# Products of the last third of each chunk cut by blocks of channels, with inverse units that wait for their own blocks and a new total order

## The chip, the cores and the metric

The kernel runs on one core of a Trainium2 chip. The metric is the device time of one execution in microseconds. An execution's time stands beside the span of its profile, which goes from the first to the last recorded instruction. Five engines run their own queues in order and wait for each other by semaphores: TensorE (PE, its weight loads shown as PEld), VectorE (DVE), ScalarE (ACT), GpSimd (POOL) and SyncE (SP), which here only issues DMAs.

## The reference

Two layers follow each other on a sequence of 2048 tokens of 640 channels (bf16):

```
k_shift = causal convolution of k with 4 taps per channel
kv      = k_shift * v
y       = irfft(rfft(kv padded to 4096) * rfft(ssm_k padded to 4096))[:2048]   # long convolution, per channel
h       = q + layernorm(q) * (y + kv * ssm_D)
out     = h + mish(layernorm(h) @ w1 + b1) @ w2                                # 640 -> 1728 -> 640
```

## The kernel before

The Fourier transforms are matmuls with constant tables, in two steps each way: 128 frequencies `f` by matmuls with cosine and sine tables, then 16 x 16 by a table `G` of its own for each `f`. The channels are taken in units of 128 ("dc", five of them) and grouped in three chunks: chunk 0 holds dc 0 and 1, chunk 1 dc 2 and 3, chunk 2 dc 4. Inside a chunk four channels form a group and four groups form a block of 16 channels, so chunks 0 and 1 have 16 blocks and chunk 2 has 8. The buffers `V` (transform of kv), `K` (transform of the filter) and `SW` (K with neighbouring partitions swapped, made by DMAs `sw0_*`, `sw1_*`, `sw2_*`) are laid out block by block, 128 frequencies x 4 groups = 512 elements for a block in a partition.

The stages, with the names that the order uses (`x` and `y` at the end of a name are the two halves of a unit):

- `k1pe`/`k1ev` and `ktpe`/`ktev` transpose the filter and k, `ktsh` shifts, `wsh` makes the small shift matrices on GpSimd, `kspe` makes k_shift in PSUM and `kv` (VectorE, L609) multiplies it by v.
- `s1kpe`/`s1kev` and `s1vpe`/`s1vev` (L558, L559) are the first forward step of filter and kv, 40 units each. They use TensorE as two tiles of 64 columns.
- `s2kpe`/`s2kev` (L658) and `s2vpe0`, `s2vpe1` with `s2vev0`, `s2vev1` (L693) are the second forward step: 43 units for the filter, 16 units for the kv of chunk 0 and 26 for that of chunks 1 and 2 together.
- `p2_c_i` (L718) multiplies SW by V and `p1_c_i` (L714) multiplies V by K in place, for piece i of chunk c. They run on VectorE or GpSimd.
- `i1pec_u`/`i1evc_u` (L751, L752) is the first inverse step, 16 + 16 + 8 units of 8 matmuls. Its result `Z` is written over `K`.
- `i2pa`, `i2pb`, `i2pc` (L809) are the second inverse step for the three chunks, 16 token tiles each. `y..a` and `y..b` take the results out, then come `wb`, `h`, `bn`, `pow`, `hc` (second layer norm), a transpose (`trpe`, or the DMA `trd`), `m1pe` (L906) with `hb` (Mish on ScalarE, L911), and `m2q`, `m2pe` (L927, L939) with `res` and `d_out`.

Every unit with a PE step allocates one of 8 PSUM banks, and its eviction (`..ev`, by ScalarE as L423 or by VectorE as L425) gives the bank back. `fz0` to `fz3` are four fillers of two 512-column matmuls on zeros, and `ln1_t` are the first layer norm's statistics of a token tile on VectorE.

Who does what, and in which order, is one list of words (`ORDER`, "name:engine"). `_schedule` walks over it and gives each operation a start time, and the instructions are emitted in the order of these times; on each engine this is the order of the list. Nothing is reordered at run time. Where GpSimd runs a product after one of VectorE, a one-column copy `turn` on GpSimd makes it wait for that product.

Three rules of the code matter to the change. In chunk 0 there are 8 pieces of 16 frequencies over all 16 blocks, in chunk 1 there are 4 pieces of 32 frequencies over all 16 blocks, and in chunk 2 there are 4 pieces of 32 frequencies over all 8 blocks. All units of the first inverse step of a chunk depend on all products of that chunk (`p_ops[c.i]`). And Z is laid out with each of its 32 rows over all channels of the chunk,

```
        Z.append(k.rearrange("p (j d) -> p j d", d=c.w))
```

so that what one unit writes is spread over the memory of all the blocks of K.

Of the kernel before, what the change touches and what calls it, by code (L numbers as in the profile page):

```python
# [26 lines left out]
d_id:s wz:v wm:t d_dr:s d_sk:s dcpe:t d_go:d d_n0:d d_n2:d k1pe0y:t warm:a k1ev0y:a d_n3:d dcev:v dq0:v k1pe0x:t k1ev0x:v cfpe:t k1pe2y:t s1kpe0_0y:t  # L27
s1kev0_0y:a s1kpe0_3y:t s1kpe0_2y:t s1kev0_3y:v s1kpe0_0x:t s1kpe0_1y:t dq3:v s1kpe0_3x:t s1kpe0_1x:t s1kpe0_2x:t dq2:v coef:a k1ev2y:a d_n1:d dq1:v
k1pe3x:t d_n4:d s1kev0_2x:a s1kev0_3x:v dq4:v d_k2:d wsh2_0:p kz:p wsh0_1:p wsh4_1:p wsh1_0:p wsh3_1:p wsh1_1:p wsh3_0:p s1kev0_1y:a k1pe1x:t k1pe1y:t
k1ev1y:a k1ev1x:v k1pe2x:t k1ev2x:v wsh4_0:p k1pe4y:t k1ev4y:v k1ev3x:v k1pe4x:t s1kev0_1x:a s1kpe1_1x:t k1pe3y:t s1kpe2_2x:t s1kev0_0x:a k1ev4x:a  # L30
d_k3:d s1kpe2_0x:t s1kev2_2x:a s1kev0_2y:a d_k0:d d_x0:d s1kpe2_0y:t s1kpe1_2x:t s1kev2_0x:a s1kpe4_3y:t s1kev2_0y:a s1kev4_3y:a k1ev3y:v s1kev1_1x:v
s1kev1_2x:v s1kpe3_0y:t s1kpe1_0y:t s1kpe1_0x:t s1kev1_0x:a s1kpe2_1y:t s1kpe3_3y:t s1kev3_0y:v s1kpe3_1y:t s1kev3_1y:a s1kev1_0y:a wsh2_1:p d_k1:d
d_g1:d d_g0:d s1kpe3_3x:t s1kev2_1y:v wsh0_0:p d_g2:d d_g7:d s1kpe2_1x:t s1kev2_1x:a s1kpe1_2y:t s1kpe1_1y:t fz2:t d_v1:d ln1_2:v s1kpe4_1y:t
s1kev4_1y:a ln1_3:v ln1p3:p ln1p2:p s1kev1_2y:v ktpe3y:t ktev3y:a s1kpe2_2y:t ktpe0y:t s1kev3_3x:a s1kev3_3y:a s1kev1_1y:v ln1_1:v fz0:t ktpe4y:t
# [20 lines left out]
s1vev2_2x:v s2kev_14y:v s1vev3_2x:v s2kpe_14x:t b1pe:t s1vev3_2y:a c_b1:a s1vpe4_3y:t s1vpe3_0y:t s2kev_14x:v s1vpe4_0x:t s1vev4_0x:a s1vev3_0y:v
p2_0_3:p p1_0_3:p d_x2:d sw0_2:d s2vpe0_6y:t s1vev4_1x:v p2_0_2:v s2vev0_6y:a s1vev4_3y:a s1vpe4_2y:t s1vpe2_2y:t s1vev4_2y:v s1vpe4_1y:t s1vpe4_2x:t
s1vev4_1y:v s1vpe3_3x:t s1vev2_2y:a s1vev3_3x:a s1vpe2_1y:t s1vev2_1y:a p2_0_7:p s1vpe3_1y:t s1vpe2_3y:t s1vev2_3y:v s1vpe2_1x:t s1vpe3_1x:t fz3:t
s1vev3_1x:a s1vev3_1y:a s1vpe2_3x:t s1vev2_3x:a s2vpe0_4y:t s1vev4_2x:a s2vpe0_4x:t s2vev0_4y:a s2vev0_4x:a s1vev2_1x:v s2vpe1_5y:t s2vpe1_6x:t
s2vpe1_8y:t s2vpe1_1x:t s2vev1_6x:a s2vev1_5y:a s2vpe1_4x:t s2vpe1_6y:t s2vpe1_3y:t s2vpe1_2y:t s2vev1_4x:a s2vpe1_1y:t p2_0_6:v sw1_0:d p1_0_7:v
p1_0_2:v p1_0_6:v s2vpe1_2x:t s2vpe1_8x:t s2vev1_6y:a s2vev1_2y:a p2_0_4:p s2vev1_8y:v sw1_1:d s2vpe1_4y:t s2vev1_1x:v s2vev1_1y:v s2vev1_3y:a  # L60
s2vev1_4y:a s2vpe1_5x:t fz1:t s2vpe1_11y:t s2vpe1_10x:t s2vev1_8x:v p2_0_5:v p1_0_4:v s2vpe1_0y:t s2vpe1_0x:t s2vpe1_3x:t s2vpe1_12x:t p1_0_5:v
s2vev1_5x:a s2vev1_2x:a s2vev1_3x:a sw2_1:d s2vpe1_11x:t s2vpe1_12y:t s2vev1_0x:a s2vev1_12x:a p2_1_1:v s2vev1_0y:a s2vpe1_9x:t p2_1_0:v p1_1_1:v
s2vev1_12y:a s2vev1_9x:a s2vev1_11x:a s2vev1_11y:a i1pe0_2x:t s2vpe1_9y:t i1pe0_7y:t s2vev1_9y:a p1_1_0:v i1pe0_5x:t s2vpe1_7x:t s2vev1_7x:a
s2vpe1_10y:t s2vev1_10y:a s2vpe1_7y:t s2vev1_7y:a i1pe0_2y:t i1pe0_0x:t i1pe0_4x:t p2_1_2:v s2vev1_10x:a i1ev0_0x:a i1pe0_5y:t p2_1_3:v p1_1_2:v
i1ev0_5x:a i1ev0_2y:a i1pe0_7x:t i1pe0_6x:t i1ev0_4x:a p1_1_3:v i1pe0_4y:t i1ev0_7x:a i1ev0_4y:a i1pe0_6y:t i1pe0_1x:t i1pe0_1y:t i1ev0_6y:a
i1ev0_2x:a i1pe0_3x:t i1ev0_7y:v i1pe0_0y:t i1pe0_3y:t i1ev0_3y:v i1ev0_1x:a i1ev0_1y:a i1pe1_4y:t i1pe1_3y:t i1ev0_0y:a i1ev1_4y:a i1ev0_5y:a
i1ev1_3y:a i1ev0_6x:a i1pe1_5x:t p2_2_3:v p2_2_2:v p1_2_3:v i1pe1_7y:t i1ev0_3x:a i1ev1_7y:a i1pe1_2y:t i1pe1_1y:t i1pe1_6x:t i1pe1_0x:t i1pe1_0y:t
i1pe1_5y:t i1ev1_5x:a i1ev1_0y:a i1ev1_1y:a i1pe1_7x:t i1ev1_7x:a i1ev1_6x:a sw2_0:d d_w11:d d_w14:d p2_2_1:v p2_2_0:v p1_2_2:v p1_2_1:v p1_2_0:v
d_t2m:d ln1_15:v d_w12:d i1pe1_4x:t i1pe1_3x:t i1pe1_6y:t i1pe2_3y:t i1ev1_4x:a d_w13:d i1ev1_0x:a i1ev1_5y:a i1pe1_2x:t i1pe2_3x:t i1ev1_2y:v
i1ev2_3x:v i1ev1_6y:v i1pe1_1x:t i1ev2_3y:a i1ev1_3x:a i1ev1_1x:v i1pe2_1y:t d_w10:d d_w2:d d_x1:d i1pe2_2x:t i1pe2_1x:t i1pe2_0x:t i1pe2_2y:t  # L70
# [222 lines left out]
def kernel(  # L293
# [698 lines left out]
```

## Time and profile before

| | before |
|---|---|
| median of 3 runs | 223.04 us (222.61 to 223.31) |
| profiled execution | 222.57 us, span 220.8 us |
| granted TensorE clock | 1.0 throughout |
| PE busy | 214.0 us, 97% of the span |
| VectorE busy | 144.1 us, 65% |
| ScalarE busy | 134.7 us, 61% |
| GpSimd busy | 73.0 us, 33% |

The shares are averages over stages of different kinds. Up to about 88 us TensorE, ScalarE and VectorE are all close to full; after about 110 us TensorE alone is. A TensorE that is busy for 97% of the span is not one that never waits: a matmul's end is modelled, and a matmul of 128 columns is shown as 220 ns long while the next one starts 55 ns later. What TensorE loses is therefore read from the distance between the starts of units of one kind.

### The profile page before, as it was taken

How to read it: one execution, taken by the hardware profiler on the slowest of the kernel's cores; microseconds unless marked ns; L12 is line 12 of the kernel's file. 1: busy time of each engine (PE TensorE's matmuls, PEld its weight loads, DVE VectorE, ACT ScalarE, POOL GpSimd, SP SyncE). 2: the span in 40 equal slices, each digit the busy share in tenths (PEclk: the TensorE clock that was granted, in tenths of full speed). 3: DMA queues.
4: the chain of work that ended last, by engine and by line, in shares of the span. 5: the costliest groups of instructions: out<-in, count | busy, mean ns of one | idle time of the engine just before them, and what ended most of it. 6: DMA issues, size and time to landing. Idle time of an engine off the chain costs nothing.

```text
span 220.8 us, 6315 instructions
## 1 busy us (share of the span) xinstructions
PE 214.0 (97%) x2626; PEld 158.3 (72%) x2626; DVE 144.1 (65%) x323; ACT 134.7 (61%) x264; POOL 73.0 (33%) x112
## 2 busy tenths in 40 slices
PE   7999999999988999999999999999999999999993
PEld 3997999898777999999776644567645444646672
DVE  0498999999999998999997999763500000020341
ACT  2699999999999999898773058600026655400000
POOL 0299983099740006025876451311000000000000
PEclk9999999999999999999999999999999999999999
DMA  6999992442999999603006300524350000000024
GB/s 216 405 415 406 423 404 96 98 93 57 286 261 277 325 390 359 200 0 62 0 0 62 62 0 0 75 46 92 89 149 1 0 3 0 0 26 7 0 82 155
DMA packets 32876, 31.03 MB, mean 141 GB/s; under 512 B 19024, under 2 KB 29264, under 8 KB 32464
## 3 DMA queue, kind: packets, MB, share of 16 engines
q1 hardware_dynamic: 32384, 30.43, 44.7%
q8 instruction: 20, 0.33, 0.6%
q10 hardware_dynamic: 368, 0.20, 0.4%
q14 instruction: 8, 0.07, 0.1%
q0 software_dynamic: 96, 0.00, 0.0%
HBM read 20.47 MB, written 2.62 MB: 105 GB/s over the span
## 4 chain that ended last, share of the span: by engine, by line
PE 79%; ACT 9%; DMA 7%; DVE 2%; issue 1%; SPq 0%
PE ps L939 26%; PE ps L906 26%; ACT uv L423 7%; DMA x<-in_A_q_dram 5%; PE ps L751 4%; PE ps L809 4%; PE ps L658 4%; PE ps L752 4%; PE ps L558 3%; DMA rn<-in_A_ssm_k_dram 2%; PE ps L605 2%; PE ps L693 2%; ACT uk L423 1%; PE ps L927 1%; PE ps L886 1%
## 5 line engine op out<-in xcount | busy, mean ns | idle before, releaser
L911 ACT ACTIVATE uv<-ps,b1s 128x512 bf16<-128x512 f32 (+1 forms) x65 | 35.8, 611 | 45.6 <-PE ps L906 37.6
L906 PE MATMUL ps<-G 128*128 128x512 bf16 (+1 forms) x325 | 58.9, 337 | 0.0
L939 PE MATMUL ps<-rn,uv 128*128 128x320 bf16 (+2 forms) x416 | 58.2, 299 | 0.0
L939 PEld LDWEIGHTS <-uv 128*128 128x128 bf16 x416 | 39.3, 98 | 17.9 <-issue 1.3
L423 ACT CAST uk<-ps 128x512 bf16<-128x512 f32 (+2 forms) x88 | 47.3, 707 | 2.7 <-PE ps L559 1.3
L906 PEld LDWEIGHTS <-G 128*128 128x128 bf16 x325 | 31.0, 98 | 24.4 <-issue 1.2
L423 ACT CAST uv<-ps 128x512 bf16<-128x512 f32 (+2 forms) x61 | 32.6, 769 | 0.0
L944 DVE TENSOR_TENSOR xa<-ps,xa 128x320 bf16<-128x320 f32 x12 | 5.8, 487 | 37.6 <-PE ps L939 37.6
L425 DVE CAST uk<-ps 128x512 bf16<-128x512 f32 (+1 forms) x35 | 21.8, 666 | 1.9 <-PE ps L559 1.4
L944 DVE TENSOR_TENSOR xb<-ps,xb 128x320 bf16<-128x320 f32 (+2 forms) x12 | 5.6, 488 | 21.0 <-PE ps L939 21.0
L751 PE MATMUL ps<-a,uv 128*128 128x128 bf16 x160 | 19.0, 219 | 0.2
L833 POOL TENSOR_TENSOR r<-ve,mhalf 128x1 f32<-128x1 f32 x16 | 9.7, 613 | 26.3 <-DVE ve L830 26.3
L751 PEld LDWEIGHTS <-uv 128*128 128x128 bf16 x160 | 17.9, 114 | 0.2 <-issue 0.2
L718 POOL TENSOR_TENSOR rn<-rn,uv 128x1024 bf16<-128x1024 bf16 x5 | 10.6, 2129 | 9.1 <-ACT uv L423 8.8
L425 DVE CAST uv<-ps 128x512 bf16<-128x512 f32 (+1 forms) x21 | 13.3, 677 | 0.1
L693 PE MATMUL ps<-uv,G 128*128 128x64 bf16 (+1 forms) x256 | 12.2, 197 | 1.2 <-issue 0.9
L658 PE MATMUL ps<-uk,G 128*128 128x160 bf16 x128 | 12.7, 230 | 0.4 <-ACT uk L423 0.3
L609 DVE TENSOR_TENSOR ra<-ps,rb 128x512 bf16<-128x512 f32 x20 | 12.5, 682 | 0.1
L693 PEld LDWEIGHTS <-G 128*128 128x128 bf16 x256 | 10.7, 96 | 2.2 <-issue 1.5
L559 PE MATMUL ps<-cst,ra 128*64 128x128 bf16 x160 | 10.9, 221 | 0.0
L558 PE MATMUL ps<-cst,ra 128*64 128x128 bf16 x160 | 10.8, 220 | 0.0
L809 PE MATMUL ps<-uk,ra 128*128 128x256 bf16 (+1 forms) x96 | 10.6, 255 | 0.0
(114 smaller groups left out, 377.3 us busy)
## 6 DMA issues: line engine op xcount, KB each, us to landing
G<-tab_g SPq DMA_DIRECT2D x8, 512.0 KB, 11.2
rn<-in_A_ssm_k_dram SPq DMA_DIRECT2D x5, 512.0 KB, 5.9
ra<-in_A_k_dram SPq DMA_DIRECT2D x4, 640.0 KB, 10.3
rb<-in_A_v_dram SPq DMA_DIRECT2D x2, 1280.0 KB, 10.2
G<-in_B_w_dram SPq DMA_DIRECT2D x5, 432.0 KB, 7.8
rn<-in_B_w_dram SPq DMA_DIRECT2D x1, 2080.0 KB, 12.6
rn<-uk SPq DMA_DIRECT2D x8, 256.0 KB, 4.2
rb<-uk SPq DMA_DIRECT2D x8, 256.0 KB, 5.0
```

Of the source, the lines that this page charges most:

```text
L423: nc.scalar.copy(o, i)
L425: nc.vector.tensor_copy(o, i)
L558: nc.tensor.matmul(ps[0:64, k, :], lhs, mc, start=True, stop=True)
L609: nc.vector.tensor_tensor(kv_w[:, m, k:32:2, 8 * h:8 * h + 8, :], ps.rearrange("p (l t d) -> p d t l", l=4, t=8), raw_v[:, 8 * h:8 * h + 8 ...
L658: nc.tensor.matmul(ps[:, o:o + 160], g_v[:, f, :], KA[:, :, f, :], start=True, stop=True)
L693: nc.tensor.matmul(ps[:, fl * n:fl * n + n], g_v[:, f0 + h * kf + fl, :], VX[x][:, :, f0 + h * kf + fl, :], start=True, stop=True)
L751: nc.tensor.matmul(pz[:, k, :], V[c.i][:, dg // 4, :, dg % 4], a12[:, 0, :], start=True, stop=False)
L809: nc.tensor.matmul(py, t2m[:, t2, ri, :], Z[c.i][:, ri * NT + t2, :], start=(ri == 0), stop=(ri == 1))
L906: nc.tensor.matmul(ph[:, 0:w], w1[:, dc, fc * P:fc * P + P], lnhT_of(u)[:, dc, 0:w], start=(dc == 0), stop=(dc == NDC - 1))
L911: nc.scalar.activation(hb_of(u)[:, fc, 0:w], rt.tile[:, 0:w], ACT.Mish, bias=b1s[:, fc:fc + 1], scale=1.0)
L939: nc.tensor.matmul(po[:, 0:d1 - d0], hb_of(u)[:, fc, tl * P:(tl + 1) * P], w2[:, fc, d0:d1], start=False, stop=(fc == NFC - 2))
L944: nc.vector.tensor_tensor(x, rt.tile[:, 0:d1 - d0], x, ALU.add)
```

## The change

The change cuts the last pieces of each chunk by blocks instead of by frequencies, lets each half unit of the first inverse step wait for the products of its own block alone, and lays Z out block by block, so that a half unit writes over the K block that it alone replaces. The second inverse step then reads its 256 (or 128) channels as runs of 16 that stand 512 elements apart. The rest is a new list `ORDER`: the same 411 TensorE operations and the same DMAs, in another order, and with other engines for some evictions and products. A piece in `PIECES` gives the first and last frequency and the first and last block, and `p_by` collects the products of each block.

```diff
+PIECES = [
+    [(16 * i, 16 * i + 16, 0, 16) for i in (0, 1, 2, 3)] + [(64, 96, 0, 8), (64, 96, 8, 16)] + [(16 * i, 16 * i + 16, 0, 16) for i in (6, 7)],
+    [(0, 32, 0, 16), (32, 64, 0, 16)] + [(64, 128, 4 * i, 4 * i + 4) for i in range(4)],
+    [(0, 64, 0, 4), (0, 64, 4, 8), (64, 96, 0, 8), (96, 128, 0, 8)],
+]
...
-        Z.append(k.rearrange("p (j d) -> p j d", d=c.w))
+        Z.append(k.rearrange("p (b j d) -> p b j d", j=2 * NT, d=16))
...
-        npf = (16, 32, 32)[c.i]
-        for i in range(P // npf):
-            f0, f1 = i * npf, (i + 1) * npf
+        for i, (f0, f1, b0, b1) in enumerate(PIECES[c.i]):
+            parts = [(max(b, b0) - b, min(b + t.shape[1], b1) - b, b, t) for b, t in SW[c.i] if b < b1 and b + t.shape[1] > b0]
...
+                    v = V[c.i][:, b0:b1, f0:f1, :]
+                    eng.tensor_tensor(v, v, K[c.i][:, b0:b1, f0:f1, :], ALU.mult)
...
+                for x, y, b, t in parts:
+                    k = t[:, x:y, f0:f1, :]
+                    eng.tensor_tensor(k, k, V[c.i][:, b + x:b + y, f0:f1, :], ALU.mult)
...
+            for b in range(b0, b1):
+                p_by[c.i][b] += [p2, p1]
...
-                ev(e, Z[c.i][:, :, d0:d0 + 4 * n].rearrange("p j (g l) -> p j g l", l=4), ps.rearrange("p (g j l) -> p j g l", g=n, l=4))
-            o_pe, o_ev = unit(f"i1pe{c.i}_{gi}", f"i1ev{c.i}_{gi}", 0.9, EV, 1024, p_ops[c.i] + [d_a12], pe, evf)
+                ev(e, Z[c.i][:, 2 * gi + h].rearrange("p j (g l) -> p j g l", l=4), ps.rearrange("p (g j l) -> p j g l", g=4, l=4))
+            o_pe, o_ev = unit(f"i1pe{c.i}_{gi}", f"i1ev{c.i}_{gi}", 0.9, EV, 1024, (p_by[c.i][2 * gi] + [d_a12], p_by[c.i][2 * gi + 1] + [d_a12]), pe, evf)
...
-                        nc.tensor.matmul(py, t2m[:, t2, ri, :], Z[c.i][:, ri * NT + t2, :], start=(ri == 0), stop=(ri == 1))
+                        nc.tensor.matmul(py, t2m[:, t2, ri, :], Z[c.i][:, :, ri * NT + t2, :], start=(ri == 0), stop=(ri == 1))
```

From the new order, the parts that the prediction uses. VectorE around the products (`:v` only, with `:p` for GpSimd's):

```
before  p2_0_6 p1_0_7 p1_0_2 p1_0_6 s2vev1_8y s2vev1_1x s2vev1_1y s2vev1_8x p2_0_5 p1_0_4 p1_0_5 p2_1_1 p2_1_0 p1_1_1 p1_1_0
        p2_1_2 p2_1_3 p1_1_2 p1_1_3 i1ev0_7y i1ev0_3y p2_2_3 p2_2_2 p1_2_3 p2_2_1 p2_2_0 p1_2_2 p1_2_1 p1_2_0 ln1_15
        i1ev1_2y i1ev2_3x i1ev1_6y i1ev1_1x i1ev2_1x i1ev2_2x i1ev2_2y y0a
before  GpSimd: p2_0_0 p1_0_0 p2_0_1 p1_0_1 p2_0_3 p1_0_3 p2_0_7 p2_0_4 gate
after   s2vev0_4y p2_0_7 s2vev1_11y s2vev1_7y s2vev0_5y s2vev1_4y s2vev1_8y p2_0_5 p1_0_7 p2_0_4 p1_0_6 p1_0_5 p1_0_4 s2vev1_11x
        p2_1_0 p1_1_0 p2_1_1 p2_1_2 p1_1_1 p1_1_2 p2_1_4 p2_1_5 i1ev1_0x p1_1_4 p1_1_5 p2_1_3 p2_2_3 p1_1_3
        p2_2_1 p2_2_2 p1_2_3 p1_2_1 p1_2_2 p2_2_0 p1_2_0 i1ev1_7x i1ev1_4y i1ev1_5y i1ev2_0y i1ev2_0x y0a
after   GpSimd: p2_0_2 p1_0_2 p2_0_3 p1_0_3 p2_0_0 p2_0_1 p1_0_1 p1_0_0 p2_0_6 gate
```

SyncE's DMAs up to the last token load:

```
before  d_n0 d_n2 d_n3 d_n1 d_n4 d_k2 d_k3 d_k0 d_x0 d_k1 d_g1 d_g0 d_g2 d_g7 d_v1 d_v0 d_g6 d_g4 d_g5 d_g3 d_a12
        sw0_0 sw0_1 sw0_3 d_x2 sw0_2 sw1_0 sw1_1 sw2_1 sw2_0 d_w11 d_w14 d_t2m d_w12 d_w13 d_w10 d_w2 d_x1
after   d_n0 d_n1 d_n2 d_n3 d_n4 d_k3 d_x0 d_a12 d_k2 d_k0 d_k1 d_g2 d_g3 d_g4 d_g1 d_v1 d_v0 d_g0 d_g7 d_g5 d_g6
        sw0_1 sw0_0 sw2_0 sw0_3 sw0_2 sw1_0 sw1_1 d_t2m sw2_1 d_w13 d_w11 d_w14 d_w12 d_w10 d_w2 d_x2 d_x1
```

TensorE's inverse units and their neighbours:

```
after   .. s2vpe1_12y fz1 fz0 s2vpe1_10y s2vpe1_9y fz3 s2vpe1_7x s2vpe1_8x s2vpe1_6y i1pe0_5y i1pe0_0x i1pe0_4y s2vpe1_6x i1pe0_2x
        s2vpe1_5x (11 more of i1pe0) i1pe1_0x 1x 0y 1y i1pe0_7y i1pe1_4x 5x 6x 6y 5y 7x 3x 7y 2x 3y 2y 4y
        i1pe2_2x 3x 2y 1x 0y i2pa0 i1pe2_1y 0x 3y i2pb0 i2pa1 i2pa8 i2pb1 i2pc0 ..
before  .. the last four s2vpe1 between the first i1pe0, then i1pe0, i1pe1 and i1pe2 in turn, i2pa0 i1pe2_0y i2pb0 i2pa1 i2pa2 i2pb1 i2pc0 ..
```

More of the change, by code (lines that the diff above doesn't have):

```diff
@@ L31 @@
[L31 to L34, printed above, removed]
@@ L55 @@
[L55 to L58, printed above, removed]
@@ L59 @@
[L59 to L70, printed above, removed]
@@ L572 @@
     p_ops = [[] for _ in CHUNKS]
+    p_by = [[[] for _ in range(c.ng // 4)] for c in CHUNKS]
     ks_pe_all, kv_ops, s1_k = [], [[] for _ in range(NDC)], {}
```

140 lines of the change are left out of this document (77 added, 63 removed).

## The prediction

> **What bounds the kernel now.** I read the page first (engine shares and slices), then the busy times by stage, then the timelines of ScalarE, VectorE, TensorE and GpSimd where the inverse step begins. Of these times, "start to start" means the distance between two starts in a timeline, since the durations shown overlap.
>
> The busy times by stage (columns: stretch, its length, then busy us and instructions of PE, PEld, DVE, ACT, POOL, then clock, DMA share, GB/s):
>
> ```profile
> 30.00:62.00 32.00, 31.06 (x720) 28.32 (x718) 31.75 (x54) 31.65 (x68) 19.84 (x17) 1.00 0.58 155
> 62.00:72.50 10.50, 9.79 (x181) 8.90 (x181) 10.50 (x16) 10.50 (x24) 2.31 (x2) 1.00 1.06 281
> 72.50:89.50 17.00, 17.00 (x287) 16.77 (x286) 16.41 (x28) 16.02 (x33) 3.64 (x5) 1.00 1.04 357
> 89.50:110.00 20.50, 20.50 (x223) 18.18 (x220) 19.24 (x57) 18.09 (x47) 9.41 (x18) 1.00 0.19 53
> 110.00:220.80 110.80, 107.40 (x700) 62.79 (x698) 45.83 (x128) 34.93 (x58) 17.80 (x39) 1.00 0.19 42
> ```
>
> From 30 to 89.5 us VectorE and ScalarE are as full as TensorE: every result of TensorE is evicted by one of them. After 110 only TensorE is full. So I cut the span at the first `i2pc0` matmul, 89.45, which needs every eviction of the first inverse step. What follows is 131.3 us, and the distances between TensorE's starts there show no wait beyond some 0.1 us a place; only an `i2pc0` that starts earlier or later can move the end much.
>
> ScalarE's timeline (columns: start, busy us, engine, line, operation, count, idle before):
>
> ```profile
> 14.32 4.99 ACT L423 CAST uk<-ps 128x512 bf16<-128x512 f32 x10
> ...
> 8.30 0.59 ACT L423 CAST uk<-ps 128x512 bf16<-128x512 f32 x1 [1.33 <-PE ps L559]
> ...
> 30.35 6.58 ACT L423 CAST uk<-ps 128x480 bf16<-128x480 f32 x14 [0.50 <-DVE ra L609]
> 36.67 0.75 ACT L423 CAST uv<-ps 128x512 bf16<-128x512 f32 x1
> ...
> 57.33 15.66 ACT L423 CAST uv<-ps 128x512 bf16<-128x512 f32 x33
> 72.61 14.79 ACT L423 CAST uk<-ps 128x512 bf16<-128x512 f32 x29
> 87.67 0.59 ACT L423 CAST uk<-ps 128x512 bf16<-128x512 f32 x1 [0.27 <-PE ps L752]
> 88.78 0.59 ACT L423 CAST uk<-ps 128x512 bf16<-128x512 f32 x1 [0.53 <-PE ps L752]
> ```
>
> Prices: start to start a 512-column eviction costs ScalarE 0.478 (ten from 14.32, the next row at 19.11), a 480-column one 0.451 (fourteen from 30.35 to 36.67). From 72.61, though, 29 take 15.06 where 13.9 are due: the inverse evictions do wait, for TensorE.
>
> VectorE and GpSimd at the products, and TensorE at the first unit of chunk 1:
>
> ```profile
> 61.61 1.89 DVE L714 TENSOR_TENSOR uv<-uv,uk 128x1024 bf16<-128x1024 bf16 x3
> 65.68 1.09 DVE L718 TENSOR_TENSOR rn<-rn,uv 128x1024 bf16<-128x1024 bf16 x1
> 70.31 2.35 DVE L714 TENSOR_TENSOR uv<-uv,uk 128x2048 bf16<-128x2048 bf16 x2
> 74.99 2.35 DVE L714 TENSOR_TENSOR uv<-uv,uk 128x2048 bf16<-128x2048 bf16 x2
> ...
> 64.10 2.12 POOL L718 TENSOR_TENSOR rn<-rn,uv 128x1024 bf16<-128x1024 bf16 x1 [0.25 <-DMA rn<-uk]
> ...
> 77.45 0.22 PE L751 MATMUL ps<-a,uv 128*128 128x128 bf16 x1
> ```
>
> A 1024-column product costs VectorE 0.602 (three from 61.61, the next start at 63.42), a 2048-column one 1.136, GpSimd 2.13. The last product of chunk 1 ends at 74.99 + 2.35 = 77.34 and the first `i1pe1` matmul starts 0.11 later: that is the wait which the change cuts. It is small, for TensorE, at 0.447 a unit, had only just finished chunk 0's 16 units.
>
> **The change part by part.** I add up each queue to two marks, at the prices above (others: 0.909 for ScalarE's and 0.60 for VectorE's transposes of 1024, 0.598 and 0.565 for VectorE's evictions of 512 and 480, 0.598 for a `kv`, 1.04 for an `ln1`).
>
> Mark A, the last forward kv eviction (`s1vev`), is at 61.95. ScalarE's queue up to it sums to 52.19 before and 51.80 after: one transpose of k1 and two `s1kev` and two `s2kev` more (0.909 + 0.956 + 0.902), one `ktev` (0.909), four `s2vev0` (1.912) and `c_b1` (0.340) less: -0.39. VectorE: 50.38 to 48.67, -1.71 (`p2_0_2` goes to GpSimd, fewer evictions). TensorE: two fillers of 0.536 move behind the mark, the other units differ by a few, 52.96 to 51.54, and 31 becomes 27 changes between two 64-column tiles and the full array, which show as some 0.11 of distance each: -1.86 in all. ScalarE gains least, so A is -0.4. Its bounds: ScalarE idles 1.33 before 8.30, for the first `s1kpe`; after, `coef` and a 0.909 transpose stand ahead of that eviction and can fill up to 1.0 of it, so -1.4; and nothing gained, if its waits grow by the 0.4.
>
> From A to `i2pc0`, 27.50 before. ScalarE has 25.70 of work there (2 `s2vev0`, 22 `s2vev1`, 31 `i1ev`), so it waits 1.8. After: 2 + 21 + 34, 26.68, for it takes three inverse evictions more from VectorE. VectorE's queue falls from 27.06 to 26.14. Whether ScalarE waits less is decided by TensorE and the products. After A, VectorE begins at about 60.8 (`s2vev0_4y`), and its sums give `p1_0_5` at +7.1 (67.9; before 67.98), `p1_1_2` at +14.1 (74.9), `p1_1_4` 76.5, `p1_1_5` 77.1, `p1_1_3` 79.7, `p1_2_2` 82.7, `p1_2_0` 83.9. TensorE starts `i1pe0_5y` behind `p1_0_5`; 15 units of chunk 0 and two `s2vpe1` (0.215) bring it to 75.1, where `i1pe1_0x` finds blocks 0 to 3 done since 74.9, 2.4 ahead of the old 77.34. `i1pe1_4x` comes five units later, 77.4 (products 76.5), `i1pe1_3x` at 80.0 (79.7), `i1pe2_2x` at 82.7 (82.7), `i1pe2_1x` at 84.1 (83.9), the last unit ends at 86.6. So the products are just in time each time, and ScalarE's own queue, A's 61.55 + 26.68 = 88.2, ends last; with 0.3 of waits 27.0 instead of 27.5: -0.5. Bounds: no waits, -0.8; the old 1.8 kept, +1.0.
>
> The new waits: VectorE's `i1ev1_0x` stands ahead of `p1_1_4`, so if `i1pe1_0x` is late, `p1_1_4` and all behind it are too; by the sums VectorE arrives at 76.1 and the matmuls are done at 75.8.
>
> Smaller parts. Chunk 1's last two `p1` of 2048 become four of 1024: 4 x 0.602 - 2 x 1.136 = +0.14 on VectorE, which ends 1 us before ScalarE: hidden. [...] `i1ev` writes 512 elements in a row in place of runs of 16: `s1kev` writes so already and costs the same 0.478 and 0.598, so nothing. `i2p` reads runs of 16 elements: L658 reads runs of 4 at 69.7 ns for 160 columns (0.435 ns each), `i2p` 109 ns for 256 (0.426), so nothing, and at the rate of L658 at most 0.18 for 20,480 columns. SyncE: `d_t2m` is moved ahead of `sw2_1` (up to 2.7 later, by 80.12 - 77.42 between landings; the swaps landed by 75.21, `p2_2_3` needs its one at 78.5, so 0.6 is left) and `d_x2` (54.09 to 60.39) behind `d_w2`, some 2.5 more ahead of `d_x1`, which landed at 93.13 and is first read at about 99. `b1pe` moves past the full stretch, its price is in the sums.
>
> From `i2pc0` on the work is the same and 22 tile changes stay 22. ScalarE gets `c_b1`, four `y..b` of 0.16 and an earlier `lnx7` (0.81), VectorE loses as much; TensorE's cover is its lead of several banks, and if it is gone up to 0.8 shows. VectorE's way to the first transposes of 512 tokens sums to 29.2 in place of 29.8. I take 0, with 0 to +0.8 as bounds.
>
> Sum: -0.4 - 0.5 + 0 = -0.9. The profiled execution of before took 222.57, 0.47 under the median; on the median this is 223.04 - 0.9 = 222.1. Bounds: -2.2 (220.8) and +1.4 (224.4).
>
> **The rivals.** (1) ScalarE bounds it with its old waits. Its queue to the last inverse eviction is 0.59 longer (77.89 to 78.48), and it lost 11.5 us besides before. If it loses as much, the time is 223.6. For it: VectorE and TensorE gain where they do not end last. Against it: 1.33 and 1.8 of the waits have reasons that the new order touches.
>
> (2) GpSimd holds VectorE off. The 65.68 product took 1.09, not 0.68, and ended when GpSimd's of 64.10 had ended, at 66.22. After, GpSimd has nine products in place of eight before the inverse step; eight from 45 on end near 62.3, while VectorE's `p2_0_7` stands at 61.0: 1.3 late, all products shift, TensorE's inverse step ends 1.2 later, 87.8 plus eviction: about 222.8. [...]
>
> (3) Slower: VectorE stands at `ln1_2` for `d_x0`. It has 5 operations fewer ahead of it, and comes 3.0 earlier than 17.05, at 14.05. `d_x0` has two quarters of k (1.58 each, 14.80 to 16.38 to 17.96) fewer ahead: 17.96 - 3.16 = 14.8. But if transfers in flight share the engines and it lands at 17.96 as before, VectorE waits 3.9 where it waited 0.93, with four evictions and as many banks behind it; less its 1.2 of spare work up to the last `s1kev` (19.73 to 18.52) that is +1.8: 224.8. It decides from a landing at about 16.2 on.
>
> That the change does not do what it says is out: in the built program `i1pe0_5y` waits for `p1_0_5`, `i1pe1_0x` for `p1_1_2`, `i1pe2_2x` for `p1_2_2`, each with later products still open.
>
> **How the numbers follow.** Chances: forecast 0.50 (its own range 221.1 to 222.9), rival 1 0.17, rival 2 0.13, rival 3 0.20. A difference under 0.3% (0.67 us) can hardly be told from none. The forecast gives 0.42 faster and 0.08 same, rival 1 half same and half slower, rival 2 0.05 faster, 0.05 same, 0.03 slower, rival 3 is slower: 0.47, 0.22, 0.31. The range goes from 220.9 (the lower bound) to 224.5, leaving out most of rival 3 and little else.
>
> **What would show it.** Right: mark A near 61.5, the first chunk 1 unit near 75, more than 2 before the last product of chunk 1, ScalarE without a gap from A to about 88, `i2pc0` near 88.5, and the rest 131.3 again. Wrong: `i2pc0` at 89.5 or later, a gap of VectorE at `ln1_2` of over 2 us, a product of chunk 0 of over 1 us on VectorE, or a first half that gains and a rest that is longer.

## The result, and the profile after

The changed kernel took 222.82 us (median of 22 executions, 222.01 to 223.17) beside 223.38 for the kernel before (median of 22, 222.3 to 223.85): ratio 0.9974, 95% interval 0.9963 to 0.9985. It is faster by 0.56 us where 0.9 was forecast. The prediction held that under 0.3% (0.67 us) a difference can hardly be told from none; 22 executions of each do tell this one. Two further comparisons gave 0.9979 (0.9963 to 0.9995) and 0.9961 (0.9943 to 0.9979). Medians and ratios here and below leave out slow executions, over 1.5% above the fastest of their kernel (one of warm8, two each of before_warm8 and warm8_again). The profiled execution of after took 223.11, its span is 221.3.

The busy times by stage of the kernel after, columns as in the prediction:

```profile
30.00:62.00 32.00, 31.70 (x744) 29.40 (x739) 31.75 (x55) 31.50 (x68) 21.92 (x16) 1.00 0.53 141
62.00:72.50 10.50, 9.83 (x186) 9.01 (x187) 10.40 (x18) 10.50 (x24) 2.31 (x2) 1.00 1.04 275
72.50:89.50 17.00, 17.00 (x289) 16.70 (x287) 16.42 (x27) 17.00 (x36) 3.47 (x5) 1.00 1.04 345
89.50:110.00 20.50, 20.50 (x221) 18.20 (x219) 19.53 (x58) 18.32 (x50) 9.44 (x21) 1.00 0.31 98
110.00:221.30 111.30, 107.99 (x705) 63.20 (x702) 46.29 (x126) 32.53 (x58) 20.89 (x40) 1.00 0.18 42
```

ScalarE was busy for 16.02 of the 17.0 us from 72.5 to 89.5, and is now for all 17.00. Its timeline in the kernel after shows no gap from mark A to the first `i2pc0`:

```profile
58.73 13.38 ACT L428 CAST uv<-ps 128x512 bf16<-128x512 f32 x28
...
73.71 15.98 ACT L428 CAST uk<-ps 128x512 bf16<-128x512 f32 x32
89.88 2.24 ACT L428 CAST rb<-ps 128x512 bf16<-128x512 f32 x5 [0.19 <-PE ps L815]
```

The evictions in this stretch start 0.45 (480 columns) or 0.477 (512) apart where nothing holds them, and are shown 0.61 to 0.96 long; a wait that is shorter than this overlap shows as no gap. The 26.68 us of work that the prediction sums up for ScalarE from A on took 27.26, so 0.6 of waits are left where the kernel before had 1.8.

VectorE and TensorE in the timeline of the kernel after, at chunk 1 (L718 is `p1`, L722 `p2`, L758 the inverse step):

```profile
74.91 1.82 DVE L718 TENSOR_TENSOR uv<-uv,uk 128x2048 bf16<-128x2048 bf16 x2
76.65 1.28 DVE L722 TENSOR_TENSOR rb<-rb,uv 128x1024 bf16<-128x1024 bf16 x2
77.87 0.69 DVE L430 CAST uk<-ps 128x512 bf16<-128x512 f32 x1
...
80.88 0.68 DVE L718 TENSOR_TENSOR uv<-uv,uk 128x1024 bf16<-128x1024 bf16 x1
...
77.01 0.22 PE L758 MATMUL ps<-a,uv 128*128 128x128 bf16 x1
```

`p1_1_2` ends at 74.91 + 1.82 = 76.73, the first unit of chunk 1 starts at 77.01, and the chunk's last product ends at 80.88 + 0.68 = 81.56: the unit starts 4.5 us ahead of that end. The waits by blocks do what they say.

Yet the first `i2pc0` of this profile starts at 89.75, 0.30 later than before. The cause stands at the other end, in TensorE's timeline; first the kernel before:

```profile
1.24 3.85 PE L467 MATMUL ps<-hc 128*128 128x512 bf16 x11 [1.24 <-DVE warm L458]
5.04 0.24 PE L483 MATMUL ps<-d_row,cst 32*128 32x5 bf16 x4
5.21 1.24 PE L631 MATMUL ps<-cst,rn 128*128 128x128 bf16 x16
```

and the kernel after:

```profile
1.25 4.88 PE L472 MATMUL ps<-hc 128*128 128x512 bf16 x11 [1.25 <-DVE warm L463]
6.06 0.27 PE L488 MATMUL ps<-d_row,cst 32*128 32x5 bf16 x4
6.26 1.60 PE L637 MATMUL ps<-cst,rn 128*128 128x128 bf16 x16
```

The same 11 warm-up products take 3.85 and 4.88, the same 16 transposes 1.24 and 1.60. Product by product, the warm-up starts are 0.43 apart up to a moment and 0.21 from then on; in the kernel after it falls among the transposes, whose starts go from 0.107 to 0.063 apart. Worked out from the one mixed distance, that moment is 3.9 before and about 7.3 after. The clock records that lie in the traces agree: the first one, of full clock, begins at 3.91 and at 7.29. Ahead of it there is no record, and the views print 1.00 there. So the granted clock of "1.0 throughout" that the kernel before was said to have leaves out a start at half speed.

### The profile page after: what moved, and what is told of

It is laid out like the page before. It is cut to its first block, busy times and chain, and to the rows that moved or that the text cites. A ratio compares the mean times of both kernels' runs of the same rounds, so it can differ in the third digit from the quotient of the medians.

```text
span 221.3 us, 6290 instructions
## 1 busy us (share of the span) xinstructions
PE 215.1 (97%) x2626; PEld 159.3 (72%) x2626; DVE 143.0 (65%) x318; ACT 132.9 (60%) x267; POOL 77.8 (35%) x115
## 4 chain that ended last, share of the span: by engine, by line
PE 88%; ACT 9%; DVE 1%; issue 1%; DVEq 0%
PE ps L945 26%; PE ps L912 26%; PE ps L563 6%; ACT uv L428 5%; PE ps L758 4%; PE ps L759 4%; PE ps L815 4%; ACT uk L428 3%; PE ps L592 3%; PE ps L637 2%; PE ps L472 2%; PE ps L664 2%; PE ps L699 2%; PE ps L933 1%; PE ps L564 1%; PE ps L892 1%
## 5 line engine op out<-in xcount | busy, mean ns | idle before, releaser
L917 ACT ACTIVATE uv<-ps,b1s 128x512 bf16<-128x512 f32 (+1 forms) x65 | 35.3, 610 | 45.7 <-PE ps L912 45.6
L428 ACT CAST uk<-ps 128x512 bf16<-128x512 f32 (+2 forms) x95 | 49.6, 725 | 0.7 <-PE ps L664 0.5
L428 ACT CAST uv<-ps 128x512 bf16<-128x512 f32 (+2 forms) x56 | 30.4, 779 | 0.0
L430 DVE CAST uk<-ps 128x512 bf16<-128x512 f32 (+1 forms) x28 | 17.8, 666 | 3.5 <-PE ps L564 3.1
L758 PE MATMUL ps<-a,uv 128*128 128x128 bf16 x160 | 19.0, 219 | 0.0
L758 PEld LDWEIGHTS <-uv 128*128 128x128 bf16 x160 | 17.8, 113 | 0.0
L430 DVE CAST uv<-ps 128x512 bf16<-128x512 f32 (+1 forms) x26 | 16.2, 674 | 0.1
L722 POOL TENSOR_TENSOR rn<-rn,uv 128x1024 bf16<-128x1024 bf16 x5 | 10.6, 2131 | 9.5 <-DVE uv L430 9.4
L664 PE MATMUL ps<-uk,G 128*128 128x160 bf16 x128 | 12.2, 230 | 0.0
L428 ACT CAST rb<-ps 128x128 bf16<-128x128 f32 (+1 forms) x29 | 10.8, 437 | 1.0 <-PE ps L815 0.9
L564 PE MATMUL ps<-cst,ra 128*64 128x128 bf16 x160 | 11.0, 222 | 0.0
```

The lines of the kernel that those rows point to most:

```text
L428: nc.scalar.copy(o, i)
L430: nc.vector.tensor_copy(o, i)
L564: nc.tensor.matmul(ps[64:128, k, :], lhs, ms, start=True, stop=True)
L664: nc.tensor.matmul(ps[:, o:o + 160], g_v[:, f, :], KA[:, :, f, :], start=True, stop=True)
L758: nc.tensor.matmul(pz[:, k, :], V[c.i][:, dg // 4, :, dg % 4], a12[:, 0, :], start=True, stop=False)
L917: nc.scalar.activation(hb_of(u)[:, fc, 0:w], rt.tile[:, 0:w], ACT.Mish, bias=b1s[:, fc:fc + 1], scale=1.0)
```

## Experiments

Theory: the gain comes from the waits by blocks (T1). Rivals: from the new order alone (T2), or the pieces cost what the waits give (T3); and, for the later start, that it belongs to the execution (S1) or to the change (S2).

All profiles are read by the same marks: F, the first filter product (`s1kpe`); A; the first `i2pc0`; the end. Times in us; "median" is of the timed executions of that kernel, and each ratio is to the kernel before on the same chip.

| profile | F | F to A | A to i2pc0 | i2pc0 to end | median |
|---|---|---|---|---|---|
| before | 7.85 | 54.10 | 27.50 | 131.30 | 223.38 |
| before again | 7.94 | 54.43 | 28.08 | 131.27 | 223.48 |
| before, third | 8.32 | 53.71 | 27.53 | 131.30 | (222.65, one) |
| after | 9.25 | 53.23 | 27.26 | 131.56 | 222.82 |
| after again | 8.75 | 53.25 | 27.26 | 131.60 | 222.96 |
| after, third | 8.80 | 53.24 | 27.26 | 131.59 | (222.66, one) |
| after, fourth | 8.88 | 53.27 | 27.36 | 131.56 | 222.74 |
| newcode_oldorder | 8.45 | 54.73 | 27.77 | 131.40 | 223.77 |
| oldcode_neworder | 8.48 | 53.27 | 32.48 | 131.62 | 227.89 |
| earlynew_oldcode | 8.05 | 53.34 | 29.43 | 131.30 | 224.58 |
| latenew_newcode | 8.44 | 53.76 | 27.85 | 131.44 | 223.06 |
| dose_scalar | 9.21 | 53.25 | 29.11 | 131.58 | 224.93 |
| dose_vector | 8.31 | 53.34 | 28.66 | 131.59 | 224.17 |
| dose_early_scalar | 9.05 | 55.09 | 27.36 | 131.59 | 224.88 |
| dose_early_tensor | 8.88 | 54.37 | 27.27 | 131.60 | 223.89 |
| no_fillers | 9.08 | 53.24 | 27.27 | 131.59 | 222.78 |
| warm8 | 7.89 | 53.57 | 27.26 | 131.61 | 222.26 |
| warm8_again | 7.90 | 53.50 | 27.47 | 131.61 | 222.24 |
| before_warm8 | 8.11 | 54.89 | 27.50 | 131.31 | 223.53 |
| warm5 | 9.85 | 54.26 | 27.29 | 131.61 | 224.62 |

**Both kernels again.**

> The kernel before, once more, for its own spread and for its start. Time 223.2 to 223.5 (the median of its 22 runs is 223.38). Theory S1 (the later start of the profile after belongs to the execution profiled): the first filter products start anywhere from 7.8 to 9.3 here, not at 7.85 as in the first profile. Theory S2 (it belongs to the order and its DMA queue): they start at 7.8 to 8.0 again.

> The changed kernel once more. Time 222.6 to 223.1, ratio about 0.997. S1 (start is a matter of the execution): first filter products anywhere from 7.8 to 9.3, and where they start at 7.9 the span is about 1 us under 221.3. S2 (start belongs to the new order): they start at 9.0 to 9.4 again, and the last evictions of the v transform, the first i2pc0 and the end come where they did (62.5, 89.7, 221.3) within 0.3.

> The kernel before in one more execution under the profiler, for the moment at which the warm-up products go from 0.43 to 0.21 us. S1: anywhere from 4.1 to 7.4. S2: 4.0 to 5.3, as in the four profiles of the old early order.

> The changed kernel in one more execution under the profiler. S1: the warm-up products' moment anywhere from 4.1 to 7.4. S2: 5.9 or later, as in the two profiles of this kernel. From the first filter product to the end 212.0 to 212.2 in either case.

The changed kernel repeats to 0.1 us in every stretch behind F; only F moves. The kernel before does not repeat: F to A and A to `i2pc0` vary by 0.7 and 0.6. In the second profile TensorE stood among the units of v's second forward step (L693); its timeline there:

```profile
61.00 0.56 PE L693 MATMUL ps<-uv,G 128*128 128x64 bf16 x13
63.06 1.12 PE L693 MATMUL ps<-uv,G 128*128 128x64 bf16 x23 [1.51 <-issue]
```

"issue" is a wait for nothing that the profile shows; in the first profile the same gap is 0.93. The 0.02 MB packet of the instruction queue ahead of the gap starts between 60.5 and 61.0 here and between 59.5 and 60.0 there, and in the four profiles with such a gap (the three of before and latenew_newcode) the gap ends 1.4 to 1.6 after the packet has landed. That TensorE waited there for its own program is the author's guess from these times; no run shows it.

The moment of full speed came at 3.9, 4.1 and 4.9 in the three profiles of before, and at 7.3, 5.7, 5.8 and 6.2 in the four of after. Up to the end of the 11 products TensorE is given the same work in both. Yet the earliest moment came 2.7 us behind the first product (1.24) and the latest, of after, 6.0 (1.25), 3.4 apart; in the four profiles of after alone they are 1.6 apart. No run shows what sets the moment.

Nine more of the profiles below have the 11 products. Two with the old early part of the list give 5.1 and 5.1, and seven with the new one 4.3, 4.9, 5.2, 6.1, 6.8, 6.9 and 7.2. So the moment does vary by execution under either order, as S1 has it, and the new order does not always start late, as S2 had it. Yet all five moments of the old order lie under nine of the eleven of the new one, which chance alone would bring in about 1 of 150 draws. The change probably makes a late moment more frequent; by what, no run shows.

**Waits and order, one without the other.**

```diff
 # newcode_oldorder: the changed kernel, with the list ORDER of before; chunk 1's products in the order of the blocks that its units need
-... p2_1_2 s2vev1_10x .. p2_1_3 p1_1_2 .. p1_1_3 ..
+... s2vev1_10x .. p2_1_4 p1_1_4 p2_1_3 p1_1_3 .. p2_1_5 p1_1_5 p2_1_2 p1_1_2 ..
 # oldcode_neworder: the kernel before, with the new list; chunk 1's products ahead of its first unit
-... p1_1_1 p1_1_2 .. p2_1_4 .. i1ev1_0x p1_1_4 p1_1_5 p2_1_3 .. p1_1_3 ..
+... p1_1_1 p2_1_3 p1_1_2 p1_1_3 .. i1ev1_0x ..
```

> The new pieces, the waits by blocks and the in-place layout under the order of the kernel before; chunk 1's products stand in the order in which the old unit order needs their blocks (8 to 11, 4 to 7, 12 to 15, 0 to 3). T1 (the waits by blocks bring the gain): the first unit of chunk 1 starts about 1.5 to 2 us before the last product of that chunk instead of 0.11 after it, and the time falls by 0.3 to 0.6 (ratio 0.997 to 0.9985). T2 (the new order brings it, by dividing the work otherwise between the queues): the units start earlier but ScalarE's queue still ends the stage, so the first i2pc0 and the time stay within 0.2 of before (ratio 0.999 to 1.001). T3 (the new pieces cost more than the waits give): 0.2 to 0.4 slower, ratio 1.001 to 1.002.

> The old pieces, whole-chunk waits and old layout under the new order; only chunk 1's product instructions are brought forward in VectorE's queue, ahead of the first inverse unit of that chunk, since the old waits need them all there. T1 (the waits by blocks bring the gain): the first unit of chunk 1 starts right after the chunk's last product, at 80 or later instead of 77.0, the first i2pc0 comes 1 to 2 us later, and the time is 0.5 to 1.5 above the kernel before (ratio 1.002 to 1.007). T2 (the new order brings it): ratio 0.996 to 0.999, like the changed kernel.

The waits without the order bring nothing: 1.0024 (1.0003 to 1.0045), near the size that T3 gave. That the pieces cost it is not shown, for the stretch behind A, 27.77, lies among the 27.50 to 28.08 of before, and what is longer is F to A, 54.73. The first unit of chunk 1 now starts 1.04 ahead of the end of the chunk's last product (78.66 and 79.70), but that end comes 16.5 behind A instead of 15.4 to 16.0: VectorE waited 0.49 ahead of `p2_1_4` for an eviction that the wider piece needs, and a pair of half pieces takes 1.33 (75.02 to 76.35). ScalarE's waits near the end stay as they were before; its timeline in newcode_oldorder:

```profile
89.09 0.59 ACT L464 CAST uk<-ps 128x512 bf16<-128x512 f32 x1 [0.27 <-PE ps L795]
90.20 0.59 ACT L464 CAST uk<-ps 128x512 bf16<-128x512 f32 x1 [0.53 <-PE ps L795]
```

The order without the waits costs 1.0217 (1.0185 to 1.0249), far more than T1's 0.5 to 1.5 us. TensorE's timeline and the busy times of oldcode_neworder:

```profile
76.50 0.22 PE L788 MATMUL ps<-a,rn 128*128 128x128 bf16 x1
79.85 0.25 PE L787 MATMUL ps<-a,uv 128*128 128x128 bf16 x1 [3.13 <-DVE uv L750]
...
81.09 0.31 PE L787 MATMUL ps<-a,uv 128*128 128x128 bf16 x1
81.20 0.31 PE L788 MATMUL ps<-a,xa 128*128 128x128 bf16 x1
```

```profile
76.60:79.80 3.20, 0.12 (x3) 0.00 (x0) 3.19 (x4) 2.89 (x6) 0.00 (x0) 1.00 1.03 392
79.80:83.20 3.40, 3.09 (x28) 2.96 (x29) 1.81 (x4) 0.16 (x1) 0.00 (x0) 0.57 0.21 77
```

TensorE waits 3.13 for the chunk's last product, and then runs at half speed: the starts are 0.11 apart in place of 0.055, the mean granted clock of that window is 0.57, and by the clock records half clock lasts from 80.27 to 83.68. The wait is paid once more by half: 3.41 us at half speed cost an estimated 1.7. The mean clock of all six executions of this kernel is 0.982 to 0.992. The stretch is 32.48 in place of 27.3.

**Half of the order.** Both lists do nearly the same work up to the last `s1vev`, so the lists can be joined there.

```diff
 # earlynew_oldcode (code of before) and latenew_newcode (code of after)
-ORDER = one list
+ORDER = list 1 up to its last s1vev, then what is left of list 2 in its own order   (new + old, and old + new)
```

> The code of the kernel before (old pieces, whole-chunk waits, old layout); the order is the new one up to the last eviction of the v transform and the old one for all that is left. From the first filter product to that eviction the old order took 54.1 and 54.4 in two profiles, the new one 53.2 in two. Theory E (the early part of the new order carries the gain, the waits don't): that stretch takes 53.2 to 53.3 here, the stretch from there to the first i2pc0 27.5 to 28.1 as in the kernel before, and the ratio is 0.996 to 0.998. Theory W (what is taken out of the early stretch is paid back later unless chunk 1's units can start by blocks): the early stretch is as short, the next one 28.3 to 29.3, and the ratio 0.9995 to 1.002.

> The new pieces, waits by blocks and layout; the order is the old one up to the last eviction of the v transform and the new one for all that is left. Theory E: the first stretch takes 54.1 to 54.5 (GpSimd's and the other early work unchanged), the stretch to the first i2pc0 27.0 to 27.3, the rest 131.6, and the ratio is 0.9985 to 1.001. Theory W (the late part with its waits by blocks carries the gain): that stretch falls to 26.0 to 26.6, since three evictions of the first half of v and their products are done already, and the ratio is 0.994 to 0.998.

earlynew_oldcode: theory W, and more than it named. The early stretch is 53.34, as short as in the changed kernel, but the next one is 29.43 and the time 1.0054 (1.0035 to 1.0074), over W's 1.002. VectorE's first product behind A waited 2.14 for an eviction (its timeline, then ScalarE's):

```profile
63.05 0.69 DVE L754 TENSOR_TENSOR rn<-rn,uv 128x1024 bf16<-128x1024 bf16 x1 [2.14 <-ACT uv L459]
```

```profile
79.66 9.11 ACT L459 CAST uk<-ps 128x512 bf16<-128x512 f32 x18 [0.52 <-PE ps L788]
89.04 0.58 ACT L459 CAST uk<-ps 128x512 bf16<-128x512 f32 x1 [0.27 <-PE ps L788]
90.15 0.59 ACT L459 CAST uk<-ps 128x512 bf16<-128x512 f32 x1 [0.53 <-PE ps L788]
```

What the new list takes out of the early stretch (`b1pe`, two fillers, four evictions of v's first part) is paid behind A unless the late part is the new one too. latenew_newcode came out at 0.999 (0.997 to 1.0009), which is E's value; its stretch behind A, 27.85, was neither the 26.0 to 26.6 of W nor the 27.0 to 27.3 of E, and TensorE stood 1.49 around A in a gap put down to "issue". The short F to A comes with the early part, whatever the code; what it gains is kept only with the late part and the waits. The gain belongs to no part alone.

**What bounds the two stretches.** Work is doubled or taken out of the changed kernel, in one queue at a time.

```diff
 # dose_scalar (i1ev0_2x, 4x, 6x), dose_vector (s2vev1_4y, 8y, 11x), dose_early_scalar (s1vev1_0y, 2y, 3y): the eviction twice
+                for _ in range(2 if <one of these> else 1):
                     ev(e, ...)
 # dose_early_tensor (s1vpe1, six half units): the matmuls twice
-                for k in range(4):
+                for k in [0, 1, 2, 3] * (2 if not which and dc == 1 and gi != 1 else 1):
 # no_fillers: fz0 to fz3 left out
-    for i in range(4):
+    for i in range(0):
```

> The changed kernel with three of chunk 0's inverse evictions on ScalarE (the first halves of units 2, 4 and 6) made twice: 3 x 0.48 = 1.43 us more in ScalarE's queue between the last eviction of the v transform and the first i2pc0. If ScalarE's queue bounds that stretch: 27.27 becomes 28.6 to 28.8 and the time grows by 1.3 to 1.5 (ratio 1.006 to 1.007). If VectorE's products or TensorE bound it: 27.3 to 27.7, ratio 1.000 to 1.002.

> The changed kernel with three evictions of the second half of v on VectorE, ahead of all products of chunk 1, made twice: 3 x 0.57 = 1.7 us more in VectorE's queue in the same stretch. If ScalarE's queue alone bounds it: the stretch stays 27.2 to 27.6, ratio 0.9995 to 1.001 against the changed kernel. If VectorE's products bound it as well (units wait for blocks of chunk 2): 28.0 to 29.0, the time grows by 0.8 to 1.7.

> The changed kernel without the eight filler products of zeros (fz0 to fz3, two products of 512 columns each, 0.21 us apiece: 1.7 us of TensorE work, one pair near 20 and three between 66 and 69). If TensorE's own work bounds the two stretches: 0.3 less in the first one, up to 1.2 less in the second, time 221.5 to 222.3. If ScalarE's queue bounds the second one: it stays at 27.1 to 27.4 and the time at 222.6 to 223.0.

> The changed kernel with three of ScalarE's evictions of the v transform (second halves of units 0, 2 and 3 of block 1, near 37 to 39) made twice: 3 x 0.48 = 1.43 us more in ScalarE's queue between the first filter product and the last eviction of the v transform, which took 53.2 to 53.3 in six profiles of the new early order. Theory A1 (ScalarE's queue bounds that stretch, as my sum took it): 54.4 to 54.8. Theory A2 (TensorE's own work bounds it): 53.3 to 53.8. F is called the first filter product here: from F to the end 212.1 becomes 213.2 to 213.6 (A1) or 212.1 to 212.6 (A2).

> The changed kernel with six of TensorE's units of the v transform (block 1, all but unit 1) made twice: 6 x 0.22 = 1.3 us more TensorE work in the same stretch. A1 (ScalarE's queue bounds): 53.3 to 53.7. A2 (TensorE's work bounds): 54.3 to 54.7. Both: 0.6 to 1.0 more from each of the two doses.

Behind A, three more evictions on ScalarE cost 1.85 where their work is 1.43; they show up in the row of dose_scalar's ScalarE timeline, again without a gap:

```profile
73.69 17.83 ACT L428 CAST uk<-ps 128x512 bf16<-128x512 f32 x35
```

Taking three pairs of fillers (1.3 us) out of TensorE leaves the stretch at 27.27. So that work of TensorE does not bound it and ScalarE's queue does. Each ScalarE copy holds its bank 0.48 longer, and TensorE then stood 0.66 at each of three places: the queue's work is a lower price. dose_vector cost 1.40 for its 1.7, not the 0 to 0.3 of "ScalarE alone" and within the 0.8 to 1.7 of the rival, in part by another way: the copied evictions held banks, TensorE stood for them (0.5 and 0.4), and ScalarE waited for TensorE's next units. Late products may have a part in it too, for the first inverse unit came 8.12 behind A in place of 7.06, and only 0.11 behind the product that it needs. ScalarE's timeline of dose_vector:

```profile
67.12 4.65 ACT L428 CAST uv<-ps 128x480 bf16<-128x480 f32 x10 [0.86 <-PE ps L699]
71.99 0.56 ACT L428 CAST uv<-ps 128x480 bf16<-128x480 f32 x1 [0.22 <-PE ps L699]
```

Between F and A, 1.43 more on ScalarE cost 1.84 and 1.3 more on TensorE cost 1.12. That is neither A1 nor A2 but the third case, and more than it named: eight banks tie both queues together, and no one queue's sum is the length of the stretch.

**The start.**

```diff
 # warm8 and warm8_again (changed kernel), before_warm8 (kernel before); warm5 with range(5)
-        for _ in range(11):
+        for _ in range(8):
             nc.tensor.matmul(ps[:, 0:512], wz[:, 0:P], wz[:, P:D], start=True, stop=True)
```

> The changed kernel with 8 warm-up products instead of 11. In ten profiles the warm-up products start at 0.43 us intervals and go to 0.21 at a moment between 4.1 and 7.4 us. Theory S1 (that moment belongs to the execution and not to what is issued): the warm-up ends by 4.7, the first filter transposes wait for their load and start at 5.4 to 5.6 in every case, the first filter product comes at 7.9 to 8.7, and the median falls by 0.1 to 0.4 below the changed kernel's 222.8 to 223.0. Theory S3 (unbroken TensorE work brings the higher speed): the gap between the warm-up and the load puts it off, the first filter product comes at 9.5 or later, and the time is 0.5 to 1.5 above the changed kernel's.

> The kernel before with 8 warm-up products instead of 11, so that its start hangs on the first load and not on the moment at which TensorE's products go to 0.21 us. S1 (the start is a matter of the execution, alike for both orders): the first filter product comes at 7.6 to 7.95, from it to the end 212.9 to 213.8 as in the two profiles of before, and the median falls by 0.2 to 0.5 under the kernel before (222.8 to 223.1): 0.6 to 1.0 above warm8 of the new order (222.27). S2 (the new order starts later of itself): the median stays within 0.15 of the kernel before, since its start was early in nearly all executions, and the gap to warm8 is 1.0 to 1.3.

> The changed kernel with 5 warm-up products. S1 (the moment belongs to the execution): the warm-up ends near 3.6, the transposes wait for their load as in warm8, and the time is that of warm8 (222.1 to 222.4). S3 (unbroken TensorE work brings the higher speed): a gap of 1.4 us ahead of the load puts it off, the transposes take 0.43/0.21 = twice as long per product for several us, the first filter product comes at 9 to 10.5 and the time is 223 to 224.5.

> The changed kernel with 8 warm-up products, again, on the same chip as the changed kernel itself. If its gain is the shorter start (first filter product at 7.89 in its profile against 8.3 to 9.25 in nine profiles of the new order with 11): 222.1 to 222.4 here, 0.4 to 0.8 under the changed kernel beside it, the first filter product at 7.8 to 8.1. If the 222.27 was a lucky set of executions: within 0.25 of the changed kernel.

> The changed kernel beside it: 222.7 to 223.0; under the profiler its warm-up products go to 0.21 us at 4.9 to 7.4, the first filter product comes at 8.3 to 9.25, and from there to the end it takes 212.0 to 212.2.

TensorE's timeline of warm8, and of warm5:

```profile
1.25 3.59 PE L472 MATMUL ps<-hc 128*128 128x512 bf16 x8 [1.25 <-DVE warm L463]
5.07 0.24 PE L488 MATMUL ps<-d_row,cst 32*128 32x5 bf16 x4 [0.23 <-DMA d_row<-in_A_ssm_D_dram]
5.25 1.24 PE L637 MATMUL ps<-cst,rn 128*128 128x128 bf16 x16
```

```profile
1.25 2.32 PE L472 MATMUL ps<-hc 128*128 128x512 bf16 x5 [1.25 <-DVE warm L463]
5.34 0.24 PE L488 MATMUL ps<-d_row,cst 32*128 32x5 bf16 x4 [1.78 <-DMA d_row<-in_A_ssm_D_dram]
5.52 1.92 PE L637 MATMUL ps<-cst,rn 128*128 128x128 bf16 x16
```

With 8 products the first load sets the start, the 16 transposes take 1.24, and F is 7.89 and 7.90. With 5 there is a gap of 1.78, the transposes take 1.92, and full speed comes at about 11.9, behind the 3.9 to 7.3 of every profile with 11; all six executions took 224.36 or more. S3 is right for this break; behind the 0.23 of warm8 nothing of the kind is seen. warm8 took 222.26 (0.9962, 0.9946 to 0.9978). Beside the changed kernel on one chip, warm8_again took 222.24 and the changed kernel 222.74: 0.50 less, as the first case expected, but the means of the same executions are 222.54 and 222.62, and the intervals (0.9936 to 0.9991 and 0.9943 to 0.9979) overlap. That warm8 beats the changed kernel is not settled. And it has a price: with 8 products 6 of 32 executions, of either kernel, took 226.0 to 226.5, while with 11 none of 47 of the changed kernel was over 223.2 and none of the kernel before over 225.3. No profile caught one of these. That in them the break ahead of the load put full speed off, as in warm5, would fit and is not shown.

The old order gets nothing from 8 products (1.0029, 0.9998 to 1.006). Its median of 223.53 beside 223.40 is what S2 gave. But F came at 8.11 and A at 63.00, later than in any profile of before with 11. There the start does not set A, and neither S1 nor S2 had said so.

## Why the prediction was right or wrong

**The term that failed is mark A, -0.4, which put the time ahead of F at nothing.** The forecast had A at 61.55; it came at 62.48 in the first profile, and means of three and four profiles are 62.12 before and 62.17 after: no gain. Two things are inside.

From F on, the stretch did shrink, from 54.08 to 53.25 in the mean, -0.83, more than the "ScalarE gains least" sum and inside its bound of -1.4; the doses show why the least of three sums was the wrong size, since ScalarE and TensorE both push the end (1.84 for 1.43 of work and 1.12 for 1.3), and through the banks.

But the time ahead of F was no term of the sum at all, and no reason was given for that. F moved from 8.04 to 8.92 in the mean, +0.88, because full speed came later, and that took the -0.83 back. In the new order A follows F at 53.2 to 53.4 in all nine profiles with a start from 8.05 to 9.25 and no work added ahead of A, so a late start goes through to the end one for one. In the old order A does not follow F: six profiles with its early part and F from 7.85 to 8.45 have A at 61.95, 62.37, 63.00, 62.03, 62.19 and 63.18, in the order of their F.

How much of the +0.88 holds for the typical execution is less sure. From F to the end the profiles give 213.08 and 212.11, -0.97, near the whole forecast of -0.9. The seven profiled executions differ by 0.09 (222.91 and 222.82 in the mean) where the medians differ by 0.56, since two of the three of before (222.57 and 222.65) were quick. So the medians leave an estimated 0.97 - 0.56 = 0.4 for the start. The start of the changed kernel is no bad luck of its profiles: the times lie 1.8 above the spans and F to the end takes 212.1, so its median of 222.82 belongs to an F of about 8.9. For the kernel before this cannot be worked out, as its F to A varies. Why the later moment comes with the change stays open.

**A to `i2pc0`, -0.5: right in size.** 27.70 became 27.28 in the means, -0.42. The mechanism is the one named, as far as the runs show it: ScalarE without a gap, and 27.3 where the sum said 27.0. Its 0.3 of waits were 0.6. (Both of its sums price two evictions of 384 columns, 0.371 by the starts, as 480, 0.16 too much in each; the difference stands.) The split of chunk 1's `p1` stayed hidden: by the starts a half costs 0.602 and a whole 1.136, a fixed part of 2 x 0.602 - 1.136 = 0.07, and by the durations (0.684 and 1.215) 0.15. The times of the products were too early: `p1_0_5` ended at 69.11 for 67.9, `p1_1_2` at 76.73 for 74.9, the first `i1pe1` started at 77.01 for 75.1; 0.9 of that is A, the rest VectorE's queue. It cost nothing, for ScalarE ended last, and the unit of chunk 1 still came over 2 ahead of the last product. A rival for a part of the -0.42 is TensorE's gap put down to "issue", 0.93 to 1.51 around A in the kernel before: the kernel after has 0.77 there, which is a wait for an eviction, and latenew_newcode, with the new waits and a gap of 1.49, took 27.85. No run separates the two.

**After `i2pc0`, 0: mis-sized.** 131.29 became 131.58, +0.29 in the bounds of 0 to +0.8. Up to the first `m1pe0` the new order takes 7.62 in place of 7.47. oldcode_neworder has 7.62 and 131.62 with the old layout, so it is the order and not the strided reads; newcode_oldorder bounds these at some 0.1 (131.40). Nor is it the late part of the list alone, with which latenew_newcode takes 131.44.

**The base.** The sum stood on one execution, 222.57, with its moment of full speed at 3.9 and its TensorE gap of 0.93. The median of 22 is 0.8 above it, and 0.34 above the median of three to which -0.9 was applied. That 222.82 lies 0.7 above the forecast 222.1 is a smaller gain on a higher base. The upper bound of the sum, +1.4, holds A at -0.4; with A's own bound, nothing gained, it is +1.8.

**The rivals.** ScalarE with its old waits (rival 1, 223.6) did not come about: behind A they fell from 1.8 to 0.6. That newcode_oldorder took 223.77 says nothing on it, for ScalarE's queue there is the old one. Rival 2's 222.8 is the measured time, and by chance: GpSimd did not hold VectorE off. It ended its product of 59.73 at 61.86, VectorE's `p2_0_7` at 62.52 took 0.68, and VectorE's five evictions beside GpSimd's product of 63.54 took 2.99, which is five times 0.565 and one overlap. `d_x0` landed at 14.6, before the 16.2 from which rival 3 decides, and `ln1_2` ran at 15.59 without a wait for it.

**The signs.** Of those for being right, the first unit of chunk 1 ahead of the last product by over 2 and ScalarE without a gap came; A near 61.5, that unit near 75 and `i2pc0` near 88.5 did not. `i2pc0` at 89.5 or later was named as a sign of being wrong; it came at 89.75 in the first profile and at 89.25 to 89.51 in the other three. The rest was longer, too, by 0.29.

## What to carry to other kernels

A cut wait is worth what the order makes of it: alone it was worth nothing, and without it the order built on it lost 4.5 us, so test such a pair both ways. Sum a stretch for every queue, but price a change by doubling work in each: where eight banks tie the queues, as between F and A here (1.84 for 1.43 more on ScalarE, 1.12 for 1.3 more on TensorE), several of them bound it at once. Before forecasting a difference of 0.4%, take the base from several executions, give the time ahead of the first mark a term of its own, and ask of each order whether a late start is carried to the end.

## What was not expected of the hardware

TensorE's first products run at half speed until a moment that lay between 3.9 and 7.3 in the sixteen profiles with 11 of them, and the views print a granted clock of 1.00 all the while; the distances (0.43 and 0.21) and the start of the first clock record show it. The records of full clock last 215.04 or 218.45 us in fifteen of these sixteen, two lengths 3.41 apart. In the sixteenth, oldcode_neworder, half clock came back behind a wait of 3.13 us between two matmuls and lasted 3.41 us, there printed as a mean of 0.57. In warm5, with a gap of 1.78 near the start, full speed came at 11.9.
